# Two of ten pointwise instructions of the transform's rounds on GpSimd instead of VectorE

## The chip, the cores and the metric

The kernel runs on one core of one Trainium2 chip. The metric is device time in microseconds: the median of several runs of the same program. The engines of a core run side by side and wait for one another by semaphores: TensorE multiplies matrices (PE in the profile, with PEld for its weight loads), VectorE works element by element (DVE), ScalarE applies functions and copies (ACT), GpSimd does small general work and issues some DMAs (POOL), and SyncE issues most DMAs (SP). Each engine takes its instructions strictly in the order in which the program gives them.

## The reference

Two independent results stand side by side in the output. Part A is a recurrent attention over 64 segments of 32 rows, each with 8 memory rows that come out of the segment before. Part B is a long convolution of an input `u` (2048 x 1024) with a kernel `K` that is made from state-space parameters. The change lies in part B, where `K` comes first and the convolution is done by a Fourier transform:

```python
K = jnp.einsum('dn,dnl,dn->dl', Cc, P, dB).real
Kf = rfft(pad(K, L)); Uf = rfft(pad(u, L))      # length 4096
Yf = Uf * Kf                                     # complex product
y = irfft(Yf)[:, :, 0, :L].astype(bfloat16)
y = y.transpose(0, 2, 1) + u * Dskip
```

## The kernel before

All engine orders are written out by hand in the program; no scheduler moves anything. The kernel has three stretches.

The first (to about 455 us) makes the values of `K`, writes them to DRAM as `Kd`, transforms `u` and writes its spectrum to DRAM as `Ud`. The last writes of `Kd` (L973) are issued alternately by SyncE and GpSimd.

The second (about 456 to 712 us) is where the change lies. It goes over 16 rounds, one for each of four column quarters (`dq`, 256 columns) and four groups of frequencies (`kc`). In program order a round `b` holds:

1. TensorE makes the spectrum of `K` for round b + 1 (`spectrum`, L1059, 64 matmuls) in PSUM. One half, the even rows, stays there. ScalarE copies the other half to SBUF (`odd`, L1219 to L1221).
2. VectorE does the ten pointwise instructions of round b (`pointwise`), each over 128 x 1024 elements in f32: sum and difference of the two halves into `X` (L1227, L1228; one operand in PSUM, one in SBUF), then for the sum half (n_ = 0) and the difference half (n_ = 1) a product with the spectrum of `u` into `Y` (L1232) and a second product in place into `X` (L1233), then two instructions that complete the complex product over both halves (L1235, L1236), then sum and difference of the halves of `Y`, rounded to bf16 into `Bt`, for the back transform (L1238, twice). From L1232 on both operands lie in SBUF. `X` and `Y` have one buffer each.
3. SyncE issues loads: the spectrum of `u` for round b + 2 (`uq<-Ud`, L1033, in buffers that the products of round b must have released), then up to ten loads of `K` values for later quarters (`KT<-Kd`, L1007, while there are any), matrices for the back transform (`MI`, L1345), weights of part A (L229), and rows of `u` (`uu`, L1246).
4. From round 4 on, TensorE does two chunks of the back transform (`inverses(2)`, L1286, 32 matmuls each), which read `Bt` of a complete earlier quarter. ScalarE takes each out of PSUM (`yb`, L1302), and VectorE does two short instructions for each (L1305: `u` by `Dskip`; L1306: plus `yb`), both with operands in SBUF. The store goes out on ScalarE's queue.

After round 4, GpSimd makes the small constant masks of part A (memsets, selects at L201 to L208, a copy at L209). After round 15, eight chunks of the back transform are left; they need `Bt` of the last quarter. Beside them SyncE loads the rest of part A's weights.

The third stretch (from about 712 us to the end) is part A. Its segments depend on each other, and it streams weights from DRAM throughout.

Of the kernel before, what the change touches and what calls it, by code (L numbers as in the profile page):

```python
# [13 lines left out]
ALU = mybir.AluOpType  # L14
# [631 lines left out]
def part_b(ctx, tc, u, A_re, A_im, B_re, B_im, C_re, C_im, log_dt, Dskip, out_b, ahead, copies, residents, first_state):  # L646
# [6 lines left out]
    v, sc, gp, pe, sy = nc.vector, nc.scalar, nc.gpsimd, nc.tensor, nc.sync  # L653
# [570 lines left out]
    def pointwise(b, s_, o_):  # L1224
        kc, Bt, us = b % 4, Bs[b // 4], spectra.pop(0)
        X = pw.tile([128, 2, 2, 2, DQ], F32, name="x", tag="x")
        v.tensor_tensor(out=X[:, 0], in0=s_, in1=o_[:], op=ALU.add)  # L1227
        v.tensor_tensor(out=X[:, 1], in0=s_, in1=o_[:], op=ALU.subtract)  # L1228
        Y = pw.tile([128, 2, 2, 2, DQ], F32, name="y", tag="y")
        for n_ in range(2):  # L1230
            uc, un = (us[n_][:, :, i, :].unsqueeze(2).to_broadcast([128, 2, 2, DQ]) for i in range(2))
            v.tensor_tensor(out=Y[:, n_], in0=uc, in1=X[:, n_], op=ALU.mult)  # L1232
            v.tensor_tensor(out=X[:, n_], in0=un, in1=X[:, n_], op=ALU.mult)  # L1233
        Yc, Xc = (t_[:].rearrange("p a b c d -> p (a b) c d") for t_ in (Y, X))
        v.tensor_tensor(out=Yc[:, :, 0, :], in0=Yc[:, :, 0, :], in1=Xc[:, :, 1, :], op=ALU.subtract)  # L1235
        v.tensor_tensor(out=Yc[:, :, 1, :], in0=Yc[:, :, 1, :], in1=Xc[:, :, 0, :], op=ALU.add)  # L1236
        for j, op in ((0, ALU.add), (1, ALU.subtract)):
            v.tensor_tensor(out=Bt[:, kc, j], in0=Y[:, 0], in1=Y[:, 1], op=op)  # L1238

    NIV = 3  # L1240
    unsent = []
# [77 lines left out]
    for b in range(16):  # L1319
# [5 lines left out]
        if b == 3:  # L1325
            nxt = [load_inverse(*todo[n_]) for n_ in range(NIV)]
            pointwise(b, *now)
            ctx_h.close()
            ctx_p.close()
            ps_h = ctx.enter_context(tc.tile_pool(name="b_psh", bufs=3, space=PSUM))  # L1330
            ps_y = ctx.enter_context(tc.tile_pool(name="b_psy", bufs=2, space=PSUM))
# [4 lines left out]
        if b != 3:  # L1336
            pointwise(b, *now)
# [187 lines left out]
```

## Time and profile before

| what | value |
| --- | --- |
| median of 3 runs | 2071.01 us (2070.24 to 2071.99) |
| profiled execution, its own time | 2080.33 us |
| its span, first to last instruction | 2078.6 us |
| mean granted TensorE clock | 0.975 |
| busy in the span: TensorE, VectorE, ScalarE, GpSimd | 1877.4, 1415.5, 1047.8, 380.1 us |
| L1232, L1233 and L1238 on VectorE, 32 each | 1216, 1226 and 1221 ns mean |
| L1305 and L1306 on VectorE, 32 each | 418 and 425 ns mean |

A row of the profile names the engine, the line, the operation, output and inputs, and shapes; then comes the number of instructions and their busy time or mean. The timeline lists instructions in order of their start, in us from the span's start, and equal neighbours can be merged in one row (x4). A bracket at the end of a row tells how long the engine had been idle before it and what released it. Matmuls are pipelined, so a busy TensorE is not one at its peak.

### The profile page before, as it was taken

The numbers are of one execution on the slowest core, as the hardware profiler recorded it, in microseconds if no ns is written. First come the engines' busy times: TensorE is split into PE (matmuls) and PEld (weight loads), VectorE is DVE, ScalarE is ACT, GpSimd is POOL, SyncE is SP. The second block draws the span as 40 slices with busy tenths as digits, with TensorE's granted clock in tenths as the row PEclk, the third lists the DMA queues.
The fourth block names the chain that finished last, engine by engine and source line by source line (L and its number), as shares of the span: only waits on it lengthen the run. The fifth ranks groups of instructions, "written<-read, shape, count | busy, mean of one in ns | idle before, by whom it ended". The sixth has DMA issues, their size and how long they took to land. (4 is left out here: it accounts for less than half of the span.)

```text
span 2078.6 us, 78528 instructions
## 1 busy us (share of the span) xinstructions
PE 1877.4 (90%) x33734; PEld 1188.3 (57%) x33734; DVE 1415.5 (68%) x3352; ACT 1047.8 (50%) x1917; POOL 380.1 (18%) x748
## 2 busy tenths in 40 slices
PE   2799999977999779999999999999999999999999
PEld 1365666756888545555555555555555555555554
DVE  8689999989899346566666666656666666666650
ACT  5899999961333334444444444444444444444430
POOL 2133343452000011111111111111111111111120
PEclk8799999989999889999999999999999999999999
DMA  7697985665646999999999999999999999999991
GB/s 192 168 254 214 260 233 172 163 201 191 213 137 189 317 348 331 330 334 337 330 339 341 335 341 332 340 323 335 345 331 341 336 338 336 344 340 335 328 351 47
DMA packets 351187, 590.78 MB, mean 284 GB/s; under 512 B 108537, under 2 KB 228377, under 8 KB 348789
## 3 DMA queue, kind: packets, MB, share of 16 engines
q1 hardware_dynamic: 297016, 528.00, 75.4%
q10 hardware_dynamic: 44812, 28.26, 4.4%
q0 software_dynamic: 9008, 29.49, 4.3%
q8 instruction: 264, 4.33, 0.8%
q14 instruction: 87, 0.70, 0.1%
HBM read 530.86 MB, written 65.26 MB: 287 GB/s over the span
## 5 line engine op out<-in xcount | busy, mean ns | idle before, releaser
L365 PEld LDWEIGHTS <-a_hT 128*32 128x32 bf16 x12352 | 340.3, 96 | 294.1 <-issue 45.5
L371 ACT CAST arena<-acc 128x512 bf16<-128x512 f32 x384 | 225.1, 586 | 392.2 <-PE acc L365 333.6
L365 PE MATMUL acc<-W,a_hT 128*32 128x512 bf16 x4608 | 361.0, 382 | 0.6 <-issue 0.6
L474 PEld LDWEIGHTS <-arena 128*32 128x32 bf16 x8256 | 209.6, 96 | 110.2 <-ACT arena L460 54.7
L365 PE MATMUL acc<-wst,a_hT 128*32 128x512 bf16 x2304 | 231.9, 382 | 15.7 <-DMA wst<-WD_v 7.9
L292 DVE TENSOR_SCALAR arena<-keep 128x256 int32<-128x256 int32 (+1 forms) x512 | 176.2, 395 | 38.2 <-PE acc L365 35.1
L379 POOL COPY arena<-arena 128x128 bf16<-128x128 bf16 x128 | 37.6, 294 | 872.7 <-DMA arena<-PKd 311.4
L365 PE MATMUL acc<-MF,a_hT 128*32 128x512 bf16 x2048 | 172.5, 384 | 0.2 <-issue 0.2
L474 PE MATMUL pp<-W_o,arena 128*32 128x256 bf16 x4096 | 149.3, 275 | 5.4 <-DMA W_o<-in_A_Wo_dram 5.2
L167 PE MATMUL pro<-xTl,wsl 128*128 128x512 bf16 x512 | 123.0, 393 | 7.0 <-ACT xTl L111 4.9
L414 DVE TENSOR_REDUCE a_mx<-sc 128x4 f32<-128x160 f32 (+1 forms) x192 | 73.0, 380 | 82.4 <-ACT sc L410 82.4
L406 DVE TENSOR_REDUCE a_mx<-sc 128x4 f32<-128x160 f32 (+1 forms) x192 | 71.9, 374 | 79.5 <-PE sc L394 78.2
L1059 PEld LDWEIGHTS <-MF 128*128 128x128 bf16 x1024 | 103.1, 101 | 29.8 <-issue 8.6
L410 ACT ACTIVATE sc<-sc 128x160 f32<-128x160 f32 (+1 forms) x192 | 63.9, 333 | 108.0 <-DVE sc L407 85.1
L489 DVE COPY arena<-tr 128x512 bf16<-128x512 bf16 x64 | 27.2, 425 | 130.1 <-PE tr L376 130.1
L437 POOL TENSOR_TENSOR arena<-arena,a_BD 128x128 bf16<-128x128 bf16 x128 | 70.7, 552 | 227.7 <-DVE arena L424 204.6
L1059 PE MATMUL hps<-KT,MF 128*128 128x256 bf16 x720 | 94.7, 284 | 14.3 <-DVE x L1228 11.2
L567 ACT CAST arena<-pp 128x128 bf16<-128x128 f32 x128 | 27.7, 269 | 156.9 <-PE pp L474 156.9
L1286 PE MATMUL yp<-Bt,MI 128*128 128x256 bf16 x680 | 104.6, 274 | 0.8 <-ACT yb L1302 0.8
L1097 ACT ACTIVATE E<-pa 128x648 bf16<-128x648 f32 x128 | 91.4, 714 | 18.8 <-PE pa L1089 13.9
L460 ACT CAST arena<-pv 128x512 bf16<-128x512 f32 x128 | 75.3, 588 | 50.3 <-PE pp L444 39.7
L474 PE MATMUL pp<-wst,arena 128*32 128x256 bf16 x1536 | 77.2, 277 | 23.5 <-DMA wst<-WD_o 14.1
(313 smaller groups left out, 3976.0 us busy)
## 6 DMA issues: line engine op xcount, KB each, us to landing
wst<-WD_v SPq DMA_DIRECT2D x256, 512.0 KB
wst<-WD_k SPq DMA_DIRECT2D x192, 512.0 KB
wst<-WD_o SPq DMA_DIRECT2D x192, 512.0 KB
wst<-WD_q SPq DMA_DIRECT2D x128, 512.0 KB
Ud<-ux POOLq DMA_DIRECT2D x16, 1024.0 KB, 5.1
uq<-Ud SPq DMA_DIRECT2D x32, 512.0 KB
wsl<-in_A_Wk_dram SPq DMA_DIRECT2D x16, 512.0 KB
wsl<-in_A_Wv_dram SPq DMA_DIRECT2D x16, 512.0 KB
```

The source lines that it names most:

```text
L167: nc.tensor.matmul(a[:], lhsT=w[:, kc, 128 * j:128 * j + 128], rhs=xTl[:, kc, :, :].rearrange("p s k -> p (s k)"), start=(kc == 0), stop=( ...
L292: nc.vector.tensor_scalar(out=out.bitcast(I32), in0=in_.bitcast(I32), scalar1=0, scalar2=None, op0=ALU.bitwise_or)
L365: nc.tensor.matmul(a[32 * g:32 * g + 32, o_:o_ + rhs.shape[1]], lhsT=hT[:, kc, :], rhs=rhs, start=(kc == 0), stop=(kc == KC - 1), tile_pos ...
L371: nc.scalar.copy(out=q, in_=a[:])
L406: nc.vector.tensor_reduce(out=m_, in_=x, axis=AX.X, op=ALU.max)
L414: nc.vector.tensor_reduce(out=m_, in_=x, axis=AX.X, op=ALU.add)
L437: nc.gpsimd.tensor_tensor(out=L[:, 0].rearrange("p (a b) k -> p a b k", a=4), in0=bc(lt[:, :, 0:XL].unsqueeze(2), [128, 4, 4, XL]), in1=bc ...
L460: nc.scalar.copy(out=o, in_=p[:].rearrange("p a (g q) -> p a g q", g=4))
L474: nc.tensor.matmul(po[32 * qt:32 * qt + 32, o_:o_ + rhs.shape[1]], lhsT=oT[:, h % 4, (h % 16) // 4, :], rhs=rhs, start=False, stop=(h == 3 ...
L1059: pe.matmul(s_[r][half][:, cs, :], lhsT=MF[:, kc, 4 * rr + mc, cs, :], rhs=rhs, start=(i == 0 and mc == 0), stop=(i == 1 and mc == 3), ski ...
L1097: sc.activation(out=T["E", r, e // 4][:, lo:lo + 8 * NE].rearrange("p (i c) -> p i c", i=2), in_=T.pop(("p", r, e))[:, :, 0:4 * NE], func= ...
L1286: pe.matmul(yp[:, b, :], lhsT=m_[:, b, cs, kc, :], rhs=Bt[:, kc, j, half, c_, :], start=(kc == 0 and cs == 0 and half == 0), stop=(kc == 3 ...
```

## The change

GpSimd makes two of the ten instructions of a round: the second product of the difference half, and the difference of the halves of `Y`. To that end the difference half is taken first, and in each pair GpSimd's instruction is issued before VectorE's. In each round VectorE does L1227, L1228, the first product of the difference half, both products of the sum half, L1235, L1236 and the sum. GpSimd's product starts from `X` after VectorE's first product has read it (it is written in place), L1235 needs it, and GpSimd's difference needs L1236. The orders on the other engines are the same as before. On GpSimd's queue the first five rounds' instructions stand between the last `Kd` writes and the mask constants of part A, the others behind those constants. In the changed file the products have the lines L1233 and L1234.

```diff
         Y = pw.tile([128, 2, 2, 2, DQ], F32, name="y", tag="y")
-        for n_ in range(2):
+        Yc, Xc = (t_[:].rearrange("p a b c d -> p (a b) c d") for t_ in (Y, X))
+        for n_, eng in ((1, gp), (0, v)):
             uc, un = (us[n_][:, :, i, :].unsqueeze(2).to_broadcast([128, 2, 2, DQ]) for i in range(2))
             v.tensor_tensor(out=Y[:, n_], in0=uc, in1=X[:, n_], op=ALU.mult)
-            v.tensor_tensor(out=X[:, n_], in0=un, in1=X[:, n_], op=ALU.mult)
-        Yc, Xc = (t_[:].rearrange("p a b c d -> p (a b) c d") for t_ in (Y, X))
+            eng.tensor_tensor(out=X[:, n_], in0=un, in1=X[:, n_], op=ALU.mult)
         v.tensor_tensor(out=Yc[:, :, 0, :], in0=Yc[:, :, 0, :], in1=Xc[:, :, 1, :], op=ALU.subtract)
         v.tensor_tensor(out=Yc[:, :, 1, :], in0=Yc[:, :, 1, :], in1=Xc[:, :, 0, :], op=ALU.add)
-        for j, op in ((0, ALU.add), (1, ALU.subtract)):
-            v.tensor_tensor(out=Bt[:, kc, j], in0=Y[:, 0], in1=Y[:, 1], op=op)
+        for j, op, eng in ((1, ALU.subtract, gp), (0, ALU.add, v)):
+            eng.tensor_tensor(out=Bt[:, kc, j], in0=Y[:, 0], in1=Y[:, 1], op=op)
```

## The prediction

> **What bounds it now.** The page's slices come first: each slice is 52 us, and the rounds of the transform lie in slices 9 to 13.
>
> ```profile
> PE   2799999977999779999999999999999999999999
> DVE  8689999989899346566666666656666666666650
> ```
>
> Both engines look full there, so I cut the stretch by what happens in it (windows; busy us, granted clock, DMA share, GB/s).
>
> ```profile
> core 0: us, PE busy (x) PEld busy (x) DVE busy (x) ACT busy (x) POOL busy (x), PEclk, DMA share, GB/s
> 456.00:504.00 48.00, 34.27 (x255) 27.50 (x254) 47.06 (x40) 3.50 (x10) 20.03 (x44) 0.86 0.50 157
> 504.00:541.00 37.00, 37.00 (x341) 33.18 (x339) 25.90 (x27) 9.90 (x20) 0.35 (x1) 1.00 0.67 219
> 541.00:679.00 138.00, 132.61 (x1203) 117.66 (x1201) 131.90 (x140) 46.47 (x85) 0.00 (x0) 0.99 0.58 179
> 679.00:712.00 33.00, 23.72 (x226) 19.48 (x224) 8.40 (x22) 11.90 (x21) 0.00 (x0) 0.99 0.97 335
> ```
>
> Rounds 0 to 3 (456 to 504) are VectorE's: 47.06 of 48 us. Later rounds also do two inverse chunks; there TensorE works 13.97 us a round (580.29 to 594.26 in the timeline), VectorE 13.56 (582.60 to 596.16). TensorE is the limit, with VectorE 0.4 behind. At 540.96 VectorE had waited 8.91 us for a `uu` load, which SyncE issued at 538.67, after its `KT` loads. From 679 the weight loads fill the DMA engines (0.97), and the attention part follows in fixed order. So delay of the last rounds reaches the end, while early gain must first pass the `uu` wait.
>
> **Step 1, GpSimd's queue.** The order of instructions puts round 0's new product behind the `Kd` writes on GpSimd's queue.
>
> ```profile
> 477.03 2.33 POOL L973 DMA_DIRECT2D Kd<-KxT  x4 [1.16 <-issue]
> 479.36 0.22 POOL masks.py:197 MEMSET a_ident<- 128x128 bf16 x1
> ```
>
> The memset needs no data, yet it starts only behind the last write, at 479.4. Round 0's product will start there too; the writes wait for earlier writes, which the change does not touch. Price of one 128x1024 f32 product on GpSimd, from its two f32 forms:
>
> ```profile
> L933 POOL TENSOR_TENSOR ux<-us x64: 715/726/763, 127.2 to 456.3; 128x256 f32<-128x256 f32 x64
> L930 POOL TENSOR_TENSOR ux<-us x16: 1262/1270/1290, 124.7 to 451.8; 128x512 f32<-128x512 f32 x16
> ```
>
> 544 ns for 256 more elements is 2.12 ns each, so 1024 take 2.36 us (VectorE: 1.22). Bounds: above, four times the small form, 2.90; below, the 1.27 of the form half as long. I take the line through both rows, their nearest continuation; the broadcast operand and bf16 output have no row. Round 0's product ends at 481.8, and L1235, which needs it and is next on VectorE, moves from 463.29 to 481.8: **+18.5**. Behind it lie the rest of the round and round 1.
>
> **Step 2, the two engines in each other's way.** GpSimd ran small selects beside round 2. Durations first, then VectorE's instructions.
>
> ```profile
> L201 POOL TENSOR_SCALAR_AFFINE_SELECT a_mask<-a_mask x12: 183/190/1174, 480.2 to 482.2; 32x8 bf16<-32x8 bf16 x8, 32x24 bf16<-32x24 bf16 x4
> ```
>
> ```profile
> 483.41 1.18 POOL L205 TENSOR_SCALAR_AFFINE_SELECT a_BD<-a_BD 128x4 bf16<-128x4 bf16 x1
> 484.66 1.07 POOL L206 TENSOR_SCALAR_AFFINE_SELECT a_BD<-a_BD 128x4 bf16<-128x4 bf16 x1
> 486.99 0.29 POOL L209 COPY a_BDx<-a_BD 128x128 bf16<-128x128 bf16 x1
> ```
>
> ```profile
> 483.32 1.22 DVE L1233 TENSOR_TENSOR x<-uq,x 128x1024 f32<-128x1024 f32 x1
> 484.46 1.22 DVE L1232 TENSOR_TENSOR y<-uq,x 128x1024 f32<-128x1024 f32 x1
> 486.99 1.36 DVE L1235 TENSOR_TENSOR y<-y,x 128x1024 f32<-128x1024 f32 x1
> ```
>
> Beside L1227 and L1228, which read one operand from PSUM, a select takes 0.19 us. Beside L1232 and L1233, with both operands in SBUF, a select of 4 elements takes 1.1 to 1.2 and ends 0.05 after VectorE's instruction. L205 got in at 484.54 although the next L1232 had already started: GpSimd is served at VectorE's instruction boundary. The reverse also shows: L429, which takes 425 ns in the middle, took 1314 next to a GpSimd copy:
>
> ```profile
> L429 DVE TENSOR_TENSOR arena<-arena,a_BDx x128: 410/425/1314, 730.3 to 2013.9; 128x512 bf16<-128x512 bf16 x128
> ```
>
> So the two take turns by whole instructions; only the fixed start-up, 0.15 us on either side, hides in the wait (L1235 lost 0.14 to the 0.29 copy). GpSimd's 2.36 then holds VectorE 2.22, and a blocked 1.22 needs 1.07 after release.
>
> The Trainium skill, "SBUF — State Buffer", section "Who interferes with whom", states this as an exclusive lock for the whole instruction and speaks against this change; taking it literally, with no start-up hidden, would add 0.6 us to each round below, 7 us in all, an estimate.
>
> **A late round, from its own L1227** (0; L1228 at 1.13): product Y1 2.38 to 3.60, Y0 3.51 to 4.73. GpSimd's product is asked at 3.7, admitted at 4.73, done 6.95. VectorE's last product waits, done 8.02. L1235 8.05, L1236 9.19, the sum 10.44 to 11.66. GpSimd's difference, asked at 10.5, starts behind the sum, 11.66 to 13.88; four `uu` instructions wait for it, the first done at 14.15, and the next L1227 comes at **15.4**. Removed: two times 1.2 us. Added: two holds of 2.22, less the start-ups of 0.15 that VectorE's two blocked instructions hide. Against 13.56 before it is +1.8, against TensorE's 13.97 it is +1.4. In rounds 0 to 3 no `uu` work follows; the difference runs beside the next L1227 and L1228, and the round is 11.6 against 11.9.
>
> **The sum.** Round 0 from L1235 to the next L1227 takes 3.5 instead of 4.7, so round 1 is at 485.3 (+17.4). TensorE, long idle, restarts slowly (its spectrum from 494.29 took 9.7 instead of 7), which eats the small gain of rounds 1 to 3: +17 there. Round 4 hangs on TensorE, 11.26 after L1228 of round 3 as before: 522 (+17). Rounds 4 and 5 take 15.4 each where before they took 36.4 together, the 8.91 wait included. SyncE's loads slip too: the `uq` load behind round 2, issued at 498.67, must wait for that round's products, done at 497.0 + 8.0. With this slip of 6.4 `uu` lands near 547; it is wanted at 551 to 552, so that wait goes. Round 6 starts at 553 instead of 541.83, +11; the mask selects that now stand between rounds 4 and 5 on GpSimd cost 1 more, +12. Nine rounds at 15.4 are 138.6 against 124.95 (541.83 to 666.78): +13.6. Round 15 completes its result 13.9 instead of 11.9 after its start: +2. The weight loads hang on the `uu` stores before round 15 (+25.6), TensorE's last inverses on its result (+27.6). I take **+27**: the profiled execution's 2080.33 (its span of 2078.6 and 1.7 around it) becomes 2107. It lies 9.3 above the median of the runs, 2071.01, and as no term above depends on that, the same 27 gives **2098**.
>
> **Rivals.** (a) *Other admission*: GpSimd's difference gets in only after the four `uu` instructions and runs beside L1227 and L1228. A late round is then 13.2 on VectorE and TensorE's 13.97 decides: rounds 4 and 5 take 27.9, round 6 starts +9 with the selects, nine rounds add 0.8, and the last result comes 2 later still: +12, 2083. Against it: L205 entered at a boundary with the next instruction already issued. (b) *No collision* (these f32 operands do not exclude each other): VectorE's rounds are 9.7, with `uu` 11.4, and TensorE's 13.97 rules from round 4. Round 4 starts +15 (three rounds save some 2 in all), rounds 4 and 5 take 27.9 instead of 36.4, nine rounds add 0.8: +7, 2078. Against it: the selects above. (c) *A dearer product*: 2.90 gives 1.1 more per late round, eleven rounds, +12: 2110. (d) *Other side, not slower*: GpSimd's product starts before the `Kd` writes' waits end, and nothing collides. Rounds 0 to 3 then save 2.2 each, 8.7 in all; it decides if L1235 of round 0 starts before 465. But the `uu` load still lands at 540.96 and TensorE rules afterwards, so the 8.7 becomes wait: 2070. For it: no row shows a product behind these writes. Against it: the memset at 479.36. That the change does not do what it says is excluded: the order shows 32 instructions gone from VectorE and on GpSimd.
>
> **How the numbers follow.** Forecast 0.60 (own range 2091 to 2108: product 2.2 to 2.6), (c) 0.12, (a) 0.12, (b) 0.09, (d) 0.04, a gain from causes not seen 0.03. The range from 2081 to 2113 holds forecast, (a) and (c), and leaves out (b), (d), the gain and the tail of (c). What differs by under 0.2% (4.1 us) cannot be told from no change. Slower 0.93 (the first four), same 0.04, faster 0.03.
>
> **What would show it.** Right: a hole of 19 us on VectorE at 462 to 481 in round 0; GpSimd's products recorded at 3.2 to 3.5 us, waiting included; VectorE's second product near 3.2; the first `uu` product after a round near 2.5; L1227 every 15.4 us from round 6; no `uu` wait in round 5. Wrong: no hole (step 1 falls), GpSimd at 2.4 with VectorE at 1.22 (step 2 falls), or a shift at 680 that is gone by 760, loads having caught up.

## The result and the profile after

The changed kernel takes 2101.07 us (median of 6 runs, 2095.04 to 2106.57) against 2073.52 for the kernel before (6 runs beside it, 2070.24 to 2082.83). The ratio is 1.0114, 95% interval 1.009 to 1.0139: slower by 19 to 29 us, with 24 in the middle. The profiled execution took 2106.57 (forecast 2107), with a span of 2104.9 and a granted clock of 0.968.

The page's slices of the kernel after; the rounds lie in slices 9 to 14.

```profile
PE   2699999965997969999999999999999999999999
DVE  8689999868999536566566665666665665666650
```

VectorE's slice 9 falls from 8 to 6 and slice 10 from 9 to 8, which is all that this view shows of the hole; slices 11 to 13 are full although VectorE has fewer instructions. The windows, cut as before, tell more (busy us, granted clock, DMA share, GB/s).

```profile
456.00:504.00 48.00, 25.51 (x192) 20.27 (x191) 29.23 (x22) 3.53 (x11) 28.76 (x28) 0.78 0.43 143
504.00:541.00 37.00, 31.33 (x267) 27.27 (x268) 34.83 (x28) 6.07 (x16) 22.98 (x28) 0.91 0.67 222
541.00:679.00 138.00, 122.90 (x1088) 107.17 (x1087) 131.13 (x104) 41.28 (x75) 59.16 (x19) 0.95 0.48 151
679.00:712.00 33.00, 30.30 (x279) 27.01 (x277) 31.07 (x26) 9.73 (x19) 13.31 (x4) 1.00 0.62 197
```

In the first window VectorE falls from 47.06 us busy to 29.23: the hole. In the third it has 104 instructions where it had 140 and is just as busy (131.13 against 131.90): instructions last longer by waiting. TensorE does 1088 matmuls there instead of 1203. In the last window the rounds are still running, and DMA stands at 0.62 instead of 0.97: the weight loads have moved back.

The hole, first on GpSimd's timeline, then on VectorE's.

```profile
463.13 2.96 POOL L973 DMA_DIRECT2D Kd<-KxT  x5 [3.19 <-issue]
...
471.49 1.74 POOL L973 DMA_DIRECT2D Kd<-KxT  x3 [3.08 <-issue]
...
476.07 1.71 POOL L973 DMA_DIRECT2D Kd<-KxT  x3 [0.43 <-issue]
477.80 2.35 POOL L1234 TENSOR_TENSOR x<-uq,x 128x1024 f32<-128x1024 f32 x1
```

```profile
461.42 1.23 DVE L1234 TENSOR_TENSOR x<-uq,x 128x1024 f32<-128x1024 f32 x1
480.18 1.23 DVE L1235 TENSOR_TENSOR y<-y,x 128x1024 f32<-128x1024 f32 x1 [17.54 <-POOL x L1234]
```

GpSimd's product could have started by 461, behind VectorE's first product. It starts when the last `Kd` write is out, takes 2.35 us undisturbed (forecast 2.36), and VectorE stands still for 17.54 us. From 459.33 to 477.80 GpSimd issues 18 of these writes: 10.7 us are the issuing itself, some 0.6 us each, and 7.8 us are gaps in which the profile names nothing that was waited for ("issue").

A late round on VectorE's timeline (round 6, with the next round's first line).

```profile
551.63 1.22 DVE L1227 TENSOR_TENSOR x<-hps,osb__7959 128x1024 f32<-128x1024 f32 x1
...
554.07 2.36 DVE L1233 TENSOR_TENSOR y<-uq,x 128x1024 f32<-128x1024 f32 x2
556.46 3.27 DVE L1234 TENSOR_TENSOR x<-uq,x 128x1024 f32<-128x1024 f32 x1
559.83 1.23 DVE L1235 TENSOR_TENSOR y<-y,x 128x1024 f32<-128x1024 f32 x1
...
562.23 1.23 DVE L1238 TENSOR_TENSOR Bt<-y 128x1024 bf16<-128x1024 f32 x1
563.37 2.58 DVE L1305 TENSOR_TENSOR uu<-uu,Dsk 128x512 bf16<-128x512 bf16 x1
...
567.26 1.22 DVE L1227 TENSOR_TENSOR x<-hps,osb__8141 128x1024 f32<-128x1024 f32 x1
```

The same round on GpSimd's timeline.

```profile
555.38 3.27 POOL L1234 TENSOR_TENSOR x<-uq,x 128x1024 f32<-128x1024 f32 x1 [5.34 <-DVE y L1233]
562.27 3.40 POOL L1238 TENSOR_TENSOR Bt<-y 128x1024 bf16<-128x1024 f32 x1 [3.63 <-DVE y L1236]
```

Both instructions of GpSimd are recorded with their wait in them. The product starts beside VectorE's second L1233, is let in when that ends (556.43), and ends at 558.65; the moment it is let in is worked out, for the 2.22 us that are left are the undisturbed 2.35 less a start-up of 0.13. VectorE's own product, issued at 556.46, ends only at 559.73. The difference is let in behind VectorE's sum (563.46) and ends at 565.67, and the first `uu` product, usually 0.42 us, takes 2.58. So VectorE gives up 2.04 us for the one and 2.16 for the other, to be rid of 1.22 each.

### The profile page after: what moved, and what is told of

Read it like the earlier page. It is cut to its first block, busy times and chain, and to the rows that moved or that the text cites. A ratio compares the mean times of both kernels' runs of the same rounds, so it can differ in the third digit from the quotient of the medians.

```text
span 2104.9 us, 78559 instructions
## 1 busy us (share of the span) xinstructions
PE 1883.2 (89%) x33734; PEld 1191.2 (57%) x33734; DVE 1435.1 (68%) x3320; ACT 1047.8 (50%) x1917; POOL 484.1 (23%) x780
## 4 chain that ended last, share of the span: by engine, by line
PE 38%; DMA 22%; DVE 4%; issue 2%; ACT 2%; POOL 0%; SPq 0%; ACTq 0%; POOLq 0%; DVEq 0%
PE acc L365 21%; PE pp L474 7%; DMA wst<-WD_v 6%; DMA wst<-WD_o 6%; DMA arena<-PKd 5%; PE pe L610 3%; PE tr L376 2%; DMA wst<-WD_k 1%; PE yp L1286 1%; DMA W_o<-in_A_Wo_dram 1%; PE sc L390 1%; DMA wst<-WD_q 1%; DVE arena L432 1%; ACT arena L460 1%; DMA uu<-in_B_u_dram 1%
## 5 line engine op out<-in xcount | busy, mean ns | idle before, releaser
L365 PEld LDWEIGHTS <-a_hT 128*32 128x32 bf16 x12352 | 341.3, 96 | 298.9 <-issue 50.6
L365 PE MATMUL acc<-W,a_hT 128*32 128x512 bf16 x4608 | 362.8, 382 | 0.8 <-issue 0.7
L365 PE MATMUL acc<-wst,a_hT 128*32 128x512 bf16 x2304 | 234.0, 383 | 17.8 <-DMA wst<-WD_v 12.4
L365 PE MATMUL acc<-MF,a_hT 128*32 128x512 bf16 x2048 | 172.2, 383 | 0.0
L1059 PE MATMUL hps<-KT,MF 128*128 128x256 bf16 x720 | 94.7, 284 | 28.7 <-DVE x L1228 25.6
L489 DVE COPY arena<-tr 128x512 bf16<-128x512 bf16 x64 | 27.2, 425 | 127.8 <-PE tr L376 127.8
L365 PE MATMUL acc<-W_v,a_hT 128*32 128x512 bf16 x1280 | 93.6, 381 | 1.3 <-issue 1.3
```

The source lines that it names most:

```text
L365: nc.tensor.matmul(a[32 * g:32 * g + 32, o_:o_ + rhs.shape[1]], lhsT=hT[:, kc, :], rhs=rhs, start=(kc == 0), stop=(kc == KC - 1), tile_pos ...
L1059: pe.matmul(s_[r][half][:, cs, :], lhsT=MF[:, kc, 4 * rr + mc, cs, :], rhs=rhs, start=(i == 0 and mc == 0), stop=(i == 1 and mc == 3), ski ...
```

## The experiments

Theory: two things cost, the hole in round 0 (GpSimd's queue) and the turns of the two engines in every late round; the turns are over reads of SBUF by instructions with two operands there. Rivals: that one of the two carries it all; that handing work to GpSimd costs by itself; that what is lost or won in the rounds does not reach the end. Shifts below are against the same place in the profile of the kernel before, and "first attention matmul" is the first L365 (before: 705.45). Lines are moved by a few in kernels with added lines.

**1. Only from round 2 on.** The hole is taken out.

```diff
-        for n_, eng in ((1, gp), (0, v)):
+        for n_, eng in ((1, gp if b >= 2 else v), (0, v)):
...
-        for j, op, eng in ((1, ALU.subtract, gp), (0, ALU.add, v)):
+        for j, op, eng in ((1, ALU.subtract, gp if b >= 2 else v), (0, ALU.add, v)):
```

> Rounds 0 and 1 wholly on VectorE, GpSimd's two instructions from round 2 on, when its Kd writes are out. Theory (a stall behind GpSimd's queue, and turns by whole instructions from then on): no hole in round 0, round 2 starts at 480 as before the change, the uu wait in round 5 comes back, round 6 starts at 542 (551.6 with the full change), late rounds stay at 15.6 us, round 15 starts near 686; about 2090 us, 10 less than the full change. Rival (the stall is swallowed by later waits anyway and only the late rounds cost): 2101 as with the full change.

Measured: 2094.9 us, ratio 1.0102 (1.0059 to 1.0146). In the trace rounds 0 and 1 take 11.98 and 11.97 us, there is no hole, and a late round takes 15.62. The `uu` wait is back (round 5 to 6: 19.44), round 6 starts at 539.3, round 15 at 683.8 (+17.0), the first attention matmul at +15.0. The trace goes with the theory, 12 us less than the full change's +27.1. The median (+21 by the ratio) lies above its figure, and its interval (+12 to +30) holds the theory's +17 and the rival's +28 alike, so the time does not settle the size by itself.

**2. Only rounds 0 and 1.** The hole without the late turns.

```diff
+        for n_, eng in ((1, gp if b < 2 else v), (0, v)):
...
+        for j, op, eng in ((1, ALU.subtract, gp if b < 2 else v), (0, ALU.add, v)):
```

> GpSimd's two instructions in rounds 0 and 1 alone, all later rounds on VectorE. Theory: hole of 17.5 us on VectorE in round 0, round 2 starts at 495, round 6 near 549 (542 before, because the hole replaces the uu wait), late rounds at TensorE's 14.0 us; about +8, 2081 us. Rival (the whole loss is this stall, carried to the end): late rounds do not matter, 2099 us.

Measured: 2081.27 us, ratio 1.0053 (1.0025 to 1.008). VectorE's timeline:

```profile
478.88 1.22 DVE L1235 TENSOR_TENSOR y<-y,x 128x1024 f32<-128x1024 f32 x1 [17.81 <-POOL x L1234]
```

The hole is all there, round 6 starts at 547.9 (+6.0), and after it VectorE keeps TensorE's 13.97. Of 17.8 us lost in round 0, 8.2 are left at round 15 and 6.9 at the first attention matmul (the time says 11, with 5 to 17 as its interval): the 8.91 of the `uu` wait before was slack. The theory's figure holds, and the rival that the hole alone makes the loss falls.

**3 and 4. The product alone, and the difference alone**, from round 2 on.

Run 3, the product on GpSimd:

```diff
+        for n_, eng in ((1, gp if b >= 2 else v), (0, v)):
...
+        for j, op, eng in ((1, ALU.subtract, gp if False else v), (0, ALU.add, v)):
```

Run 4, the difference on GpSimd:

```diff
+        for n_, eng in ((1, gp if False else v), (0, v)):
...
+        for j, op, eng in ((1, ALU.subtract, gp if b >= 2 else v), (0, ALU.add, v)):
```

> Of the change, the product alone on GpSimd, from round 2 on; the difference stays on VectorE. Theory (each of the two instructions costs by itself, for its hold is longer than the time it takes off VectorE): VectorE's last product stays at 3.26 us, the first uu instruction is back at 0.42, VectorE needs 14.6 us for a late round (15.62 less 2.15 of uu wait, plus 1.14 for the difference), 0.6 more than TensorE; about 2081 us. Rival (only the blocked uu work costs, the product's wait hides in TensorE's time): late rounds 13.97, 2074 us.

> Of the change, the difference alone on GpSimd, from round 2 on; both products stay on VectorE. Theory: the first uu instruction stays at 2.57 us, the products are back at 1.22, VectorE needs 14.6 us for a late round (13.56 less 1.14 plus 2.15); about 2081 us. Rival (only the product costs, since L1235 waits for it): late rounds 13.97, 2074 us.

Measured: 2084.18 us, ratio 1.0049 (1.003 to 1.0068), and 2086.45, ratio 1.006 (1.0037 to 1.0082). A late round takes 14.55 and 14.78 us. Instructions by line, first of the kernel with the product alone, then with the difference alone (shortest, median and longest ns):

```profile
L1305 DVE TENSOR_TENSOR uu<-uu,Dsk x32: 411/419/425, 518.4 to 718.4; 128x512 bf16<-128x512 bf16 x32
```

```profile
L1305 DVE TENSOR_TENSOR uu<-uu,Dsk x32: 415/422/2576, 517.2 to 722.6; 128x512 bf16<-128x512 bf16 x32
```

The long `uu` product comes with the difference and goes without it; VectorE's long product (3.26) comes with GpSimd's product (in run 4 all 32 take 1.22 to 1.23). Each of the two alone lifts VectorE's 13.56 past TensorE's 13.97, so each alone costs. At round 15 the shifts are +9.5 and +13.3; 5.1 and 3.3 of them arise between rounds 13 and 14, from the wait that experiment 9 takes out.

**5. The next round's L1227 and L1228 before the `uu` instructions**, with the two on GpSimd from round 2 on.

```diff
+        now = combined(*then) if b + 1 < 16 else None
```

`combined` holds L1227 and L1228, here of round b + 1. It is called behind the round's sum and ahead of its `uu` instructions, so that instructions with one operand in PSUM stand beside GpSimd's difference.

> As e1_from2, and the next round's sum and difference (one operand in PSUM) are issued on VectorE ahead of the uu instructions, so that GpSimd's difference runs beside them. Theory (only instructions with both operands in SBUF take turns with GpSimd): the first uu instruction is down from 2.57 to 0.42 us, VectorE needs 13.5 us for a late round and TensorE's 13.97 rules; round 15 starts near 668, about 2074 us. Rival (GpSimd shuts out VectorE whatever its operands): the next round's sum takes 3.4 us, late rounds stay at 15.6, 2090 us.

Measured: 2074.8 us, ratio 1.0017 (0.9989 to 1.0045). VectorE's timeline, then GpSimd's:

```profile
592.16 1.23 DVE L1241 TENSOR_TENSOR Bt<-y 128x1024 bf16<-128x1024 f32 x1
593.30 1.22 DVE L1226 TENSOR_TENSOR x<-hps,osb__8667 128x1024 f32<-128x1024 f32 x1
594.43 1.21 DVE L1227 TENSOR_TENSOR x<-hps,osb__8667 128x1024 f32<-128x1024 f32 x1
595.57 0.41 DVE L1308 TENSOR_TENSOR uu<-uu,Dsk 128x512 bf16<-128x512 bf16 x1
```

```profile
592.20 3.40 POOL L1241 TENSOR_TENSOR Bt<-y 128x1024 bf16<-128x1024 f32 x1 [3.63 <-DVE y L1239]
```

GpSimd works from 593.39 to 595.60 beside two instructions of 1.22 and 1.21 that lose nothing, and the `uu` product is back at 0.41. VectorE's round is 13.28 us, under TensorE's 13.97, although its second product still takes 3.26. So here only instructions with both operands in SBUF take turns, and with the order changed the offload costs nothing that the time shows (−2 to +9 us). The first attention matmul comes at +4.6; the step from round 14 to 15 took 18.18 us, which experiment 10 brings down.

**6. GpSimd writes instead of computing.** From round 2 on GpSimd fills the two outputs with zeros, twice each, and the product and the difference are left out.

```diff
+            if eng is gp:
+                for i in range(MS):
+                    gp.memset(X[:, n_], 0.0)
...
+            if eng is gp:
+                for i in range(MS):
+                    gp.memset(Bt[:, kc, j], 0.0)
...
+    MS = 2
```

> As e1_from2, but in place of each of GpSimd's two instructions it writes zeros twice into the same tile, and reads nothing (the product and the difference are left out). Theory (the turns are taken over the read of SBUF): no wait on either side, VectorE's second product 1.22 us and first uu instruction 0.42 us, late rounds at TensorE's 14.0 us, about 2074 us. Rival (any work of GpSimd on SBUF takes turns with VectorE): GpSimd's writes recorded longer than the 1 to 1.2 us of its 128x1024 memsets at the start of the kernel, late rounds above 14.5 us, 2082 us or more.

Measured: 2076.94 us, ratio 1.0019 (0.9995 to 1.0043). GpSimd's timeline in a late round (two memsets a row), then VectorE's:

```profile
599.05 1.96 POOL L1236 MEMSET x<- 128x1024 f32 x2 [10.11 <-DVE y L1233]
600.96 1.96 POOL L1244 MEMSET Bt<- 128x1024 bf16 x2
```

```profile
600.16 1.23 DVE L1238 TENSOR_TENSOR x<-uq,x 128x1024 f32<-128x1024 f32 x1
601.49 1.23 DVE L1239 TENSOR_TENSOR y<-y,x 128x1024 f32<-128x1024 f32 x1
```

Each memset takes 0.95 us, and VectorE's instructions beside them, both operands in SBUF, keep their 1.23. The round is TensorE's 13.97. The wait for GpSimd's result is still in this kernel (L1239 reads what the memsets wrote), so neither writing on GpSimd nor the semaphores cost VectorE anything that shows, which leaves GpSimd's reading as what it waits for. The zeros do take less time than the product, so this run speaks of the turns and not of a long GpSimd instruction.

**7. The kernel before with its `uu` loads one further ahead** (four instead of three).

```diff
-            if len(todo) >= NIV:
-                nxt.append(load_inverse(*todo[NIV - 1]))
+            if len(todo) > NIV:
+                nxt.append(load_inverse(*todo[NIV]))
...
-            nxt = [load_inverse(*todo[n_]) for n_ in range(NIV)]
+            nxt = [load_inverse(*todo[n_]) for n_ in range(NIV + 1)]
```

> The kernel before the change, all pointwise work on VectorE, with the uu rows loaded four chunks ahead instead of three (six buffers as before), so that the load for the second chunk of round 5 is issued near 512 instead of 538.67. Theory (this load alone kept the rounds waiting there, and took up whatever VectorE saved in rounds 0 to 3): the wait of 8.9 us goes, round 6 starts near 533 instead of 542, TensorE's gap of 4.75 us after 542 goes too, then TensorE rules; 5 to 7 less than before, 2067 us. Rival (another load or the masks of the next stage hold the same place, or SyncE now waits longer for the uu stores): no change, 2073 us.

Measured: 2075.48 us, ratio 1.0013 (0.9992 to 1.0034): no gain, and the expectation missed. The wait did go: round 6 starts at 531.2 (−10.6), round 15 at 660.2, and the first attention matmul at −9.5. Of this, −5.1 and −3.0 are left at the first two segments of part A (taken at L489, which comes once in each), and there TensorE waits 5.5 us for a load of `WD_k` that it did not wait for in the kernel before. The window in which the rounds end:

```profile
679.00:712.00 33.00, 22.77 (x205) 17.62 (x207) 7.19 (x18) 9.56 (x16) 0.00 (x0) 0.81 1.02 369
```

The DMA engines are full (1.02, 369 GB/s), and TensorE's granted clock is 0.81 (0.99 in the kernel before). That an early end of the rounds is taken back by the loads, while a late end (experiments 1 to 4) delays these loads and stays, fits this but is not shown: later in the same profile the shift is −8.8 at the sixteenth segment and −12.8 at the end. That end measures little, for this execution (2067.52) is the lowest of the twelve, and the profiled one of the kernel before (2080.33) lies 7 above its median. What the times do show is that a gain of 9.5 us at the first attention matmul does not reach them (−2 to +7 us).

**8. Experiments 5 and 7 together.** The diffs are those of both.

> e5_reorder with the uu rows loaded four chunks ahead as in e7_uu4. Theory: VectorE's 13.3 us rounds do not help where TensorE needs 13.97, so this ends where e7_uu4 ends, near 2067 us; rounds 6 to 12 go from 13.3 to 13.97 once no backlog is left. Rival (VectorE's shorter rounds are worth something by themselves once the uu wait is gone): 3 or more below e7_uu4.

Measured: 2075.75 us, ratio 1.0005 (0.9986 to 1.0024). VectorE's rounds take 13.28 until it has caught up with TensorE, then 13.97; round 15 starts at 661.4. The first attention matmul comes at −3.5: TensorE's pace takes back VectorE's gain, and the step from round 14 to 15 takes 18.18 us here too. The expected 2067 is missed, as in experiment 7.

**9. The full change, with one copy on ScalarE.** Between rounds 13 and 14 the kernel after has a wait that the prediction had not seen. TensorE's waits from 640 to 690, then VectorE's timeline, then TensorE's:

```profile
PE yp L1286 <- DVE a_hT L1482: 10.3, 1, 10.3
```

```profile
672.85 0.18 DVE L1482 COPY a_hT<-yp 128x64 bf16<-128x64 bf16 x1
```

```profile
673.09 0.80 PE L1286 MATMUL yp<-Bt,MI 128*128 128x256 bf16 x3 [10.28 <-DVE a_hT L1482]
673.68 0.42 PE L1286 MATMUL yp<-Bt,mn 128*128 128x256 bf16 x1
```

L1482 empties the PSUM buffer `yp` of part A's first transposes (8x8, at 659). Its 0.18 us stand on VectorE behind all of round 13, TensorE needs the buffer for the next chunk and waits 10.28 us, and its matmuls then run at 0.42 us instead of 0.27 for a few us. The round takes 19.16 us instead of 15.62. In the kernel before the same round took 15.33, and 13.58 with the copy moved (experiment 11).

```diff
-        nc.vector.tensor_copy(out=hT[:, :, ahead.XM:], in_=pm)
+        nc.scalar.copy(out=hT[:, :, ahead.XM:], in_=pm)
```

> The full change, with the 128x64 copy of the first state (L1482, once, in round 13) on ScalarE instead of VectorE. Theory (the 19.16 us from round 13 to round 14 come from this copy: it stands behind round 13 on VectorE, and TensorE waits 10.28 us for it before its second chunk): TensorE's wait falls to 1 to 2.5 us, the round takes 15.6, round 15 starts 3.5 earlier, near 692, and the first matmul of the attention part near 729 instead of 732.5; about 2098 us. Rival (TensorE's wait is hidden, and that round is long for another reason): still 19, 2101 us.

Measured: TensorE's waits in the same stretch:

```profile
PE yp L1286 <- ACT a_hT L1482: 2.1, 1, 2.1
```

The round takes 15.63, round 15 starts at 691.8 (695.9 in the kernel after) and the first attention matmul comes 3.8 us earlier than in the kernel after. So the trace shows this term and its size. The time does not: 2099.61 us, ratio 1.0143 (1.011 to 1.0176), not to be told from the kernel after.

**10, 11 and 12. Versions that might beat the kernel before:** experiment 5 with this copy; the kernel before with this copy; experiment 8 with this copy. The diffs are those shown.

> e5_reorder with the copy of the first state on ScalarE. Theory: the step of 18.18 us from round 14 to 15 falls to about 14, round 15 starts near 661 instead of 665.4, before the kernel before the change does; but what is won ahead of the weight loads that fill the DMA engines from 680 on is given back there, so the time stays at 2073 to 2075. Rival (the win reaches the end): 2070 or less, below the kernel before.

> The kernel before the change with only the copy of the first state on ScalarE. Theory: the step from round 13 to 14 falls from 15.33 to 13.97, 1.4 us, which the weight loads take back; no change, 2073 to 2075 us. Rival (what e10_reorder_copy shows against the kernel before, some 4 us, comes from this copy alone): 2069 to 2071.

> e10_reorder_copy with the uu rows loaded four chunks ahead as well: no wait is left on VectorE in the rounds but TensorE's own pace. Theory: round 15 starts near 656, 5 before e10_reorder_copy, the first matmul of the attention part comes earlier, and the weight loads take back nearly all of it: 2070 to 2074 us. Rival (early rounds do count at the end): 2066 or less.

Measured: 2071.13 us, ratio 0.9981 (0.9954 to 1.0009); 2074.05, 0.9997 (0.9973 to 1.002); 2075.56, 1.0008 (0.9984 to 1.0032). The copy does what it should: the last full round takes 14.37 instead of 18.18 in run 10, and the step from round 13 to 14 takes 13.58 instead of 15.33 in run 11. The first attention matmul comes at −2.9 in run 10, −6.7 in run 11 and −0.9 in run 12, where two rounds of 15.40 and 17.82 us took back what the early `uu` loads had brought: ScalarE waited 7.34 us for a load of `KT` (its L1045 at 559.05), and behind it VectorE waited 2.03 us and TensorE 4.41 us for what ScalarE makes. All three intervals hold no change, and no version is shown to beat the kernel before.

Taken together, late starts of part A show in the time: +6.9, +7.5, +10.1 and +15.0 us in experiments 2, 3, 4 and 1 come with slowdowns of 5 to 17, 6 to 14, 8 to 17 and 12 to 30 us. Early starts do not: −9.5 us in experiment 7 and −6.7 in run 11 come with −2 to +7 and −6 to +4 us. Why is open.

## Why the prediction was right, and where only by luck

| place | before | forecast | measured |
| --- | --- | --- | --- |
| L1235 of round 0 | 463.29 | 481.8 (+18.5) | 480.18 (+16.9) |
| round 1 | 468.0 | +17.4 | 483.7 (+15.7) |
| round 4 | 505.4 | +17 | 520.3 (+14.9) |
| round 6 | 541.83 | +11 to +12 | 551.6 (+9.8) |
| nine rounds from there | 124.95 | 138.6 (+13.6) | 144.3 (+19.3) |
| last result of round 15 | 678.7 | 27.6 later | 709.9 (+31.2) |
| first attention matmul | 705.45 | 27 later, as the whole | 732.5 (+27.1) |
| whole, medians | 2073.5 beside it | +27 | +27.6 (19 to 29 by the ratio) |

**Step 1** held in kind (experiment 2 shows it alone) and was 1.6 us too large: the `Kd` writes were out at 477.8 instead of 479.4. The product's price was right to 0.01. That the writes wait for earlier writes, as the prediction has it, no run shows: more than half of the time is their issuing. The `uu` wait of round 5 went as forecast and came back as soon as the hole was taken out (experiment 1). Its load was issued at 540.12, 1.5 us later than before and not 6.4, which made no difference, since VectorE came to it only at 550.76.

**Step 2** held in every link: product at 3.27 on GpSimd, VectorE's second product at 3.27, first `uu` product at 2.58. A late round is 15.62 instead of 15.4. The 0.2 is spread over the gaps between instructions: the product is let in at 4.80 of the round instead of 4.73, L1235 starts at 8.20 instead of 8.05, the first `uu` product ends at 14.32 instead of 14.15, and the `uu` instructions take 0.06 more. From the sum's end to the end of that `uu` product it is 2.49 us, as forecast. Rival (a) asked for a difference that runs beside L1227 and L1228. That happens only when the program puts them there (experiment 5), so (a) falls. (b) falls by the recorded 3.27 against 2.35 undisturbed, (c) by the 2.35, (d) by the hole.

The Trainium skill's "SBUF — State Buffer", "Who interferes with whom", has VectorE and GpSimd exclude each other for whole instructions when VectorE has two SBUF inputs and GpSimd reads SBUF, and not when GpSimd only writes. Experiments 5 and 6 agree. Its literal price, with no start-up hidden, would make a late round 16.0; the 15.62 measured lies nearer to the 15.4.

**The sum of the nine rounds is the mis-sized term**: +19.3 instead of +13.6. Of the missing 5.7, some 2.0 are the longer round (nine times 0.22), and 3.5 are the wait in round 13 that no step had (19.16 against 15.62; experiment 9 removes it). In the profile of before that round already took 15.33 us, where its neighbours took 13.56 to 13.98. I read the ordinary rounds and carried them over to all nine.

These errors cancelled. The rounds began 2 us less late than forecast and ended 3.6 later, and of 31.2 us at the last result 27.1 reached part A. The prediction hung part A on two things, the stores before round 15 (+25.6) and the last result (+27.6). Measured, round 15 began at +29.1 and its last result came at +31.2, so the 27.1 lies below both, and that it met the 27 is luck. Behind the last result TensorE waited 4.4 us in the kernel before, 2.6 of them behind a late `uu` load, and 2.7 after; that is 1.7 of the missing 4.1, and the rest was not traced. From part A's start to the end the profiles wander by up to 14 us with part A unchanged: experiment 3 stands at +7.5 at the first attention matmul and at −6.3 at the end, though its runs are 6 to 14 slower, and experiment 6 at −2.6, at −9.9 sixteen segments after the first, and at 0 at the end. So the end of one profile does not measure a few us in the rounds; shifts up to part A and the ratios do.

The claim that an early gain must pass the `uu` wait first was half of it. Experiment 7 took that wait away and the time shows no gain; the weight loads behind the rounds are the likely second floor, which is not shown.

## What to carry to other kernels

Before a two-operand instruction goes to GpSimd, list what VectorE runs beside it: next to two SBUF operands, a 1.2 us instruction moved away cost 2.0 to 2.2 us of waiting, next to one PSUM operand nothing. Look also at what GpSimd's queue holds ahead of it: 18 DMA issues, of 0.6 us each with gaps between, held up the compute behind them by 17.5 us. And before counting a stretch's gain, ask what comes behind it: here the same few us counted when lost and not when won.

## What was not expected of the hardware

- The turn goes to the engine that waits, at once: in all twelve rounds with `uu` work (4 to 15) GpSimd's difference got in at the end of VectorE's sum (first `uu` product 2.5 to 2.6 us), although VectorE's next instruction was ready.
- A 128x1024 product with a broadcast operand took 2.35 us on GpSimd, as the line through its plain f32 forms says (2.36). The difference with bf16 output worked 2.21 us behind its admission (593.39 to 595.60), the product the same (556.43 to 558.65). A f32 memset of that size took 0.95 and did not mind VectorE at all.
- A copy of 0.18 us on a busy engine held TensorE for 10.28 us, and the matmuls behind the wait ran at 0.42 instead of 0.27 us for some 5 us.
